# Starting gate/up of three column blocks on half of the rows, with fill matmuls and the first weights in one queue

## The chip, the cores and the metric

The kernel runs on 1 core of one Trainium2 chip. The metric is device time in microseconds (us); times are given as medians. Before the change the kernel takes 1308.88 us (3 runs, 1308.24 to 1309.98).

## The reference, cut to what matters

A layer norm, a multi-head attention over a cached K and V (32 heads of 128), and a gated feed-forward part whose result gates the attention output:

```python
xn = layernorm(x)                       # x: 2048 rows x 512
s  = attention(xn @ wq, k_cache, v_cache) @ wo
gate = xn @ W_gate                      # 512 x 1792
up   = xn @ W_up
h    = (gate * (gate > 0)) * up
g    = silu(h @ W_down)
out  = x + s * g
```

Everything is bfloat16 with fp32 accumulation. The feed-forward part is computed first, then the attention. The first matmul that does useful work needs normalised and transposed rows (`xnT`) and the first columns of `W_gate` and `W_up`.

## The kernel before

Rows are handled in four groups of 512 (`Q`), each of four tiles of 128 rows. The 1792 columns of gate and up are 14 blocks (`fc`). For the first 512 rows the head normalises and transposes all four tiles before the first gate matmul. Twelve dummy matmuls run first, to have TensorE's clock up: the traces record the clock that TensorE is granted, 1.00 or 0.50 (called warm and cold, or full and half, below). In the trace of this kernel a 512-column matmul starts every 0.216 us at 1.00 and every 0.43 us at 0.50.

```python
FCS = [0, min(2, FC), min(8, FC), FC]      # weight chunks: blocks 0-1, 2-7, 8-13
...
load_x0(sp, 0); load_x0(act, 1); load_x0(sp, 2); load_x0(act, 3)
load_w(sp, Wg_sb, wg_src, sem_wg, 0)       # first gate weights: SP queue
load_w(act, Wu_sb, wu_src, sem_wu, 0)      # first up weights: ACT queue
load_w(sp, Wg_sb, wg_src, sem_wg, 1)
load_w(sp, Wu_sb, wu_src, sem_wu, 1)
...
def head_ln():
    st = ln_stats(0)
    st = ln_stats(1)
    sq01 = ln_aggr([0, 1], st)             # square root on ACT
    st = ln_stats(2)
    c01 = ln_coef([0, 1], sq01)
    n0 = ln_norm(pool, sem_nm, 0, c01)     # GpSimd
    n1 = ln_norm(pool, sem_nm, 1, c01)
    st = ln_stats(3)
    sq23 = ln_aggr([2, 3], st)
    c23 = ln_coef([2, 3], sq23)
    n2 = ln_norm(dve, sem_ln4, 2, c23)
    n3 = ln_norm(dve, sem_ln4, 3, c23)
    head_transpose(0, n0, act, sem_xa)     # 4 TensorE transposes, then one copy to xnT
    head_transpose(1, n1, act, sem_xa)
    head_transpose(2, n2, act, sem_xa)
    head_transpose(3, n3, dve, sem_xt)
...
def emit_gate_up(Q):
    for fc in range(FC):
        s = ring_acquire()                 # one of 3 pairs of PSUM banks
        if fc == 0:
            _wait_all(pe, xt_ready[Q])     # all four tiles
        if Q == 0 and fc in FCS:           # a new chunk of weights
            k = FCS.index(fc)
            pe.wait_ge(sem_wg[k].h, 16)
            pe.wait_ge(sem_wu[k].h, 16)
        for c in range(DC):                # 4 gate matmuls of 512 columns
            pe.matmul(ps_r[:, gb, :], Wg_sb[:, c, fs], xnT[:, c, qs], ...)
        # ... 4 up matmuls, relu on ACT, product hT on DVE, one ln_task for later rows
...
for _i in range(12):
    pe.matmul(ps_acc[:, 0, 0:D], warm[:, 0:128], warm[:], start=True, stop=True)
head_ln()
for Q in range(QB):
    hlast = emit_gate_up(Q)
    if Q < QB - 1:
        emit_down(Q, hlast)
# ... attention of 32 heads; then the last output projection:
while oproj_queue:
    _, g_, n_ = oproj_queue.pop(0)
    emit_M(None, None, (g_, n_))
gL = NG - 1
for n in range(NT):
    if n == 0:
        _wait(pe, t_tok(gL))               # the last DMA transposes of the attention output
    # ... 4 matmuls, product and sum on DVE, store
```

The softmax here doesn't subtract the row's maximum and nothing guards it: scores larger than these inputs give would overflow.

Of the kernel before, what the change touches and what calls it, by code (L numbers as in the profile page):

```python
# [5 lines left out]
BF16 = mybir.dt.bfloat16  # L6
F32 = mybir.dt.float32
ALU = mybir.AluOpType
ACTF = mybir.ActivationFunctionType
# [20 lines left out]
def _wait(eng, tok):  # L30
    if tok is None:
        return
    sem, val = tok
    if val <= 0:
        return
    eng.wait_ge(sem.h, val)


def _wait_all(eng, toks):
    best = {}  # L40
    for t in toks:
        if t is None:
            continue
        sem, val = t
        k = id(sem)
        if k not in best or best[k][1] < val:
            best[k] = (sem, val)
    for sem, val in best.values():
        _wait(eng, (sem, val))


def bass_recurrent_scan__mha_block_cached__glu_gated_reglu__prompt_kernel(
# [12 lines left out]
    _, S, D = A_x.shape  # L65
# [8 lines left out]
    DC = D // 128  # L74
    FC = F // 128
# [8 lines left out]
    NSLOT = 3  # L84
# [13 lines left out]
    pe = nc.tensor  # L98
    act = nc.scalar
    dve = nc.vector  # L100
    sp = nc.sync
    pool = nc.gpsimd

    with ExitStack() as es:
# [13 lines left out]
        ps_r = P_([128, 2 * NSLOT, 512], F32, "ps_r")  # L118
        ps_acc = P_([128, 2, 512], F32, "ps_acc")
        acc_bf = [ps_acc[:, k, :].bitcast(BF16) for k in range(2)]  # L120

        x_sb = S_([128, NT, D], BF16, "x_sb")
        xnT = S_([128, DC, S], BF16, "xnT")
# [9 lines left out]
        warm = S_([128, D], BF16, "warm")  # L133
# [12 lines left out]
        Wg_sb = SB_([128, DC, F], BF16, "Wg_sb")  # L146
# [47 lines left out]
        with nc.Block() as block:  # L194

            @block.tensor
            def _(_pe_eng):
# [10 lines left out]
                for b in range(2):  # L208
                    tok_pool = sem_pool.sig(pool.memset(V_sb[b][:, :, Dh:VW], 2.0))

                FCS = [0, min(2, FC), min(8, FC), FC]
                wg_src = B_W_gate.rearrange("(c p) f -> p c f", p=128)
                wu_src = B_W_up.rearrange("(c p) f -> p c f", p=128)

                def load_w(eng, dst, src, sems, k):
                    a, b_ = FCS[k] * 128, FCS[k + 1] * 128
                    if b_ > a:
                        sems[k].sig(eng.dma_start(dst[:, :, a:b_], src[:, :, a:b_]))
# [14 lines left out]
                load_x0(sp, 2)  # L233
                load_x0(act, 3)
                load_w(sp, Wg_sb, wg_src, sem_wg, 0)
                load_w(act, Wu_sb, wu_src, sem_wu, 0)
                load_w(sp, Wg_sb, wg_src, sem_wg, 1)
                load_w(sp, Wu_sb, wu_src, sem_wu, 1)
                if QB > 1:
# [58 lines left out]
                def ring_acquire():  # L298
                    s = ring_cnt[0] % NSLOT
                    ring_cnt[0] += 1  # L300
                    _wait_all(pe, ring_tok[s])
                    ring_tok[s] = []
                    return s
# [8 lines left out]
                def ln_aggr(ns, stok):  # L312
                    _wait(dve, stok)
                    for n in ns:
                        atok = sem_ln2.sig(dve.bn_aggr(mv[:, n, :], stats[:, n, :]))
                    a, b_ = ns[0], ns[-1] + 1
                    _wait(act, atok)
                    if a == 0:
                        _wait(act, warm_tok)
                    return sem_sq.sig(  # L320
                        act.activation(sqv[:, a:b_, :], mv[:, a:b_, 1:2], ACTF.Sqrt, bias=eps_sb[:]))

                def ln_coef(ns, sqtok):
                    a, b_ = ns[0], ns[-1] + 1
                    _wait(dve, sqtok)
                    rtok = sem_ln3.sig(dve.reciprocal(rstd[:, a:b_, :], sqv[:, a:b_, :]))
                    _wait(dve, rtok)
                    return sem_ln3.sig(
                        dve.scalar_tensor_tensor(nmr[:, a:b_, :], mv[:, a:b_, 0:1], -1.0, rstd[:, a:b_, :],
                                                 op0=ALU.mult, op1=ALU.mult))  # L330

                def ln_norm(eng, sem, n, ctok):
                    _wait(eng, ctok)
                    return sem.sig(
                        eng.tensor_scalar(xn_sb[:, n, :], x_sb[:, n, :], rstd[:, n, 0:1], nmr[:, n, 0:1],
                                          op0=ALU.mult, op1=ALU.add))
# [1 line left out]
                xt_ready = {Q: [] for Q in range(QB)}  # L338

                def head_transpose(n, ntok, eng, sem):  # L340
                    tp_ps = ps_r[:, n, :].bitcast(BF16)
                    if n == 0:
                        _wait(pe, tok_pool)
                    _wait(pe, ntok)
                    ins = None
                    for c in range(DC):
                        ins = pe.transpose(tp_ps[:, c * 128:(c + 1) * 128],
                                           xn_sb[:, n, c * 128:(c + 1) * 128], ident[:])
                    ptok = sem_tp.sig(ins)
                    src = tp_ps[:, 0:DC * 128].rearrange("p (c q) -> p c q", c=DC)  # L350
                    _wait(eng, ptok)
                    copy = act.copy if eng is act else dve.tensor_copy
                    ctok = sem.sig(copy(xnT[:, :, n * 128:(n + 1) * 128], src))
                    xt_ready[0].append(ctok)
                    ring_tok[n // 2].append(ctok)

                def head_ln():
                    st = ln_stats(0)
                    st = ln_stats(1)
                    sq01 = ln_aggr([0, 1], st)  # L360
                    st = ln_stats(2)
                    c01 = ln_coef([0, 1], sq01)
                    n0 = ln_norm(pool, sem_nm, 0, c01)
                    n1 = ln_norm(pool, sem_nm, 1, c01)
                    st = ln_stats(3)
                    sq23 = ln_aggr([2, 3], st)
                    c23 = ln_coef([2, 3], sq23)
                    n2 = ln_norm(dve, sem_ln4, 2, c23)
                    n3 = ln_norm(dve, sem_ln4, 3, c23)
                    head_transpose(0, n0, act, sem_xa)  # L370
                    head_transpose(1, n1, act, sem_xa)
                    head_transpose(2, n2, act, sem_xa)
                    head_transpose(3, n3, dve, sem_xt)

                ln_hold = {}

# [23 lines left out]
                sig_free = [None, None]  # L400
                hT_free = [None, None]

                def emit_gate_up(Q):
                    qs = slice(Q * NQ, (Q + 1) * NQ)
                    par = Q % 2
                    h_tok = None
                    for fc in range(FC):
                        fs = slice(fc * 128, (fc + 1) * 128)
                        s = ring_acquire()
                        gb = 2 * s  # L410
                        if fc == 0:
                            _wait_all(pe, xt_ready[Q])
                        if Q == 0 and fc in FCS:
# [3 lines that stand above are left out]
                        ins = None  # L417
                        for c in range(DC):
                            ins = pe.matmul(ps_r[:, gb, :], Wg_sb[:, c, fs], xnT[:, c, qs],  # L419
                                            start=(c == 0), stop=(c == DC - 1))  # L420
                        gtok = sem_gate.sig(ins)
                        for c in range(DC):
                            ins = pe.matmul(ps_r[:, gb + 1, :], Wu_sb[:, c, fs], xnT[:, c, qs],  # L423
                                            start=(c == 0), stop=(c == DC - 1))
                        gu_tok = sem_gu.sig(ins)
                        gk = fc % NSLOT
                        _wait(act, gtok)
                        _wait(act, gr_free[gk])
                        rtok = sem_relu.sig(act.activation(gr_sb[gk][:], ps_r[:, gb, :], ACTF.Relu))  # L429
                        _wait(dve, gu_tok)  # L430
                        _wait(dve, rtok)
                        if fc == 0:
                            _wait(dve, hT_free[par])
                        h_tok = sem_h.sig(
                            dve.tensor_tensor(hT[par][:, fc, :], gr_sb[gk][:], ps_r[:, gb + 1, :], ALU.mult)  # L435
                        )
                        gr_free[gk] = h_tok
                        ring_tok[s] = [rtok, h_tok]
                        if Q == 0:
                            ln_task(fc)  # L440
                    return h_tok

                def emit_down(Q, h_last_tok):
# [27 lines left out]

                assert DC == 4 and FC >= 4 * (QB - 1) + 1
                _wait(pe, warm_w)
                for _i in range(12):
                    pe.matmul(ps_acc[:, 0, 0:D], warm[:, 0:128], warm[:], start=True, stop=True)
                head_ln()
                ring_cnt[0] = 2
                for Q in range(QB):
                    hlast = emit_gate_up(Q)
                    if Q < QB - 1:  # L480
# [294 lines left out]
```

## Time and profile before

| | before |
|---|---|
| median of 3 runs | 1308.88 us |
| profiled span | 1309.6 us |
| TensorE busy | 98% |
| first gate matmul | 9.28 us |
| half clock near the head | 9.51 to 12.93 us |
| first matmul of the down projection in the chain of work that ended last ("the chain") | 35.30 us |
| TensorE idle before the last output projection | 6.0 us |

From the page of the kernel before, the busy times of the engines and the head of the chain that ended last:

```profile
PE 1281.4 (98%) x11744; PEld 838.4 (64%) x11964; DVE 442.6 (34%) x1190; ACT 1000.7 (76%) x1107; POOL 11.5 (1%) x23
...
PE 93%; DVE 3%; issue 2%; DMA 1%; SPq 0%; ACTq 0%; DVEq 0%
```

TensorE is the bound. Next, the timeline of the head of the kernel before; columns are start, duration, engine, line, operation, tiles, shape, count, and in brackets the idle time just before and what ended it:

```profile
1.19 5.17 PE L475 MATMUL ps_acc<-warm 128*128 128x512 bf16 x12 [1.19 <-DVE warm L230]
...
3.21 1.29 DVE L310 BATCH_NORM_STATS2 stats<-x_sb 128x6 f32<-128x512 bf16 x2 [2.07 <-DMA x_sb<-in_A_x_dram]
...
5.72 1.52 POOL L335 TENSOR_SCALAR xn_sb<-x_sb,rstd,nmr 128x512 bf16<-128x512 bf16 x2 [4.03 <-DVE nmr L329]
...
6.63 0.38 PE L347 MATMUL ps_r<-ident,xn_sb 128*128 128x128 bf16 x4 [0.27 <-POOL xn_sb L335]
...
7.29 1.18 PE L347 MATMUL ps_r<-ident,xn_sb 128*128 128x128 bf16 x12 [0.28 <-POOL xn_sb L335]
...
9.28 1.66 PE L419 MATMUL ps_r<-xnT,Wg_sb 128*128 128x512 bf16 x4 [0.81 <-DMA Wu_sb<-in_B_W_up_dram]
```

Dummies end at 6.36 us; then only transposes, until the first gate matmul at 9.28 us, which the landing of the up weights released. The windows of the kernel before (stretch, its length, busy time and count per engine, then granted TensorE clock, DMA share, GB/s) show what followed:

```profile
8.00:9.00 1.00, 0.47 (x7) 0.23 (x4) 0.44 (x2) 0.80 (x2) 0.00 (x0) 1.00 1.06 386
9.00:10.00 1.00, 0.72 (x3) 0.35 (x4) 0.00 (x0) 0.00 (x0) 0.00 (x0) 0.76 1.03 372
10.00:11.00 1.00, 1.00 (x4) 0.33 (x3) 0.00 (x0) 0.02 (x1) 0.00 (x0) 0.50 1.07 366
11.00:12.00 1.00, 1.00 (x3) 0.29 (x2) 0.00 (x0) 0.58 (x1) 0.00 (x0) 0.50 1.09 366
12.00:13.00 1.00, 1.00 (x4) 0.42 (x3) 0.31 (x1) 0.00 (x0) 0.00 (x0) 0.54 1.07 374
```

The third number from the end is the clock. It falls to 0.50 just as useful work begins: four matmuls per us instead of seven. A clock of 1.00 before 6.1 us is not a measurement: the trace's first clock record begins there, and the dummies, 0.43 us apart, show that the array was cold.

### The profile page before, as it was taken

The numbers are of one execution on the slowest core, as the hardware profiler recorded it, in microseconds if no ns is written. First come the engines' busy times: TensorE is split into PE (matmuls) and PEld (weight loads), VectorE is DVE, ScalarE is ACT, GpSimd is POOL, SyncE is SP. The second block draws the span as 40 slices with busy tenths as digits, with TensorE's granted clock in tenths as the row PEclk, the third lists the DMA queues.
The fourth block names the chain that finished last, engine by engine and source line by source line (L and its number), as shares of the span: only waits on it lengthen the run. The fifth ranks groups of instructions, "written<-read, shape, count | busy, mean of one in ns | idle before, by whom it ended". The sixth has DMA issues, their size and how long they took to land.

```text
span 1309.6 us, 27449 instructions
## 1 busy us (share of the span) xinstructions
PE 1281.4 (98%) x11744; PEld 838.4 (64%) x11964; DVE 442.6 (34%) x1190; ACT 1000.7 (76%) x1107; POOL 11.5 (1%) x23
## 2 busy tenths in 40 slices
PE   9999999999999999999999999999999999999996
PEld 3444466666666666666666666666666666666663
DVE  6333322222332332233233233223323323344546
ACT  3322389998888888888888888888888888888880
POOL 2000000000000000000000000000000000000000
PEclk9999999999999999999999999999999999999998
DMA  8500112232222322232221222222223222212202
GB/s 254 116 1 1 21 37 51 46 61 41 45 51 53 70 51 52 53 68 53 52 52 40 57 42 51 52 70 53 52 52 69 51 53 53 50 44 43 48 18 70
DMA packets 251575, 71.82 MB, mean 55 GB/s; under 512 B 238400, under 2 KB 251456, under 8 KB 251456
## 3 DMA queue, kind: packets, MB, share of 16 engines
q1 hardware_dynamic: 250640, 69.55, 25.4%
q8 instruction: 95, 1.56, 0.5%
q10 hardware_dynamic: 816, 0.52, 0.1%
q14 instruction: 24, 0.20, 0.0%
HBM read 32.77 MB, written 2.10 MB: 27 GB/s over the span
## 4 chain that ended last, share of the span: by engine, by line
PE 93%; DVE 3%; issue 2%; DMA 1%; SPq 0%; ACTq 0%; DVEq 0%
PE ps_acc L652 36%; PE ps_r L589 32%; PE ps_r L524 7%; PE ps_r L545 7%; PE ps_r L423 4%; PE ps_r L419 4%; PE ps_acc L456 4%; DVE Onorm L617 2%; DVE fin_tmp L731 1%; DMA Wu_sb<-in_B_W_up_dram 1%; PE ps_r L726 0%; DVE rz_sb L610 0%; SPq L628 0%; DMA OT_store<-Onorm 0%; ACTq L224 0%
## 5 line engine op out<-in xcount | busy, mean ns | idle before, releaser
L597 ACT ACTIVATE PT<-ps_r 128x1024 bf16<-128x1024 f32 x1024 | 952.3, 1054 | 172.8 <-PE ps_r L589 172.8
L652 PEld LDWEIGHTS ps_acc<-V_sb,PT 128*128 128x128 bf16 x8192 | 551.8, 98 | 247.9 <-DVE Onorm L617 6.1
L652 PE MATMUL ps_acc<-V_sb,PT 128*128 128x129 bf16 x8192 | 640.3, 221 | 2.5 <-DVE Onorm L617 0.4
L589 PE MATMUL ps_r<-QT_sb,KT_sb 128*128 128x512 bf16 x1844 | 565.5, 379 | 10.6
L610 DVE RECIPROCAL rz_sb<-ps_acc 128x2 f32<-128x2 f32 x256 | 42.2, 165 | 736.9 <-PE ps_acc L652 710.6
L589 PEld LDWEIGHTS ps_r<-QT_sb,KT_sb 128*128 128x128 bf16 x2048 | 159.3, 98 | 1.1 <-DVE QT_sb L535 0.4
L617 DVE TENSOR_SCALAR Onorm<-ps_acc,rz_sb 128x128 bf16<-128x128 f32 x512 | 156.1, 347 | 9.2
L524 PE MATMUL ps_r<-xnT,Wq_sb 128*128 128x512 bf16 x511 | 130.8, 379 | 0.1
L545 PE MATMUL ps_r<-Wo_sb,OT_store 128*128 128x512 bf16 x447 | 114.8, 379 | 0.1
L524 PEld LDWEIGHTS ps_r<-xnT,Wq_sb 128*128 128x128 bf16 x512 | 50.1, 98 | 60.5
L535 DVE CAST QT_sb<-ps_r 128x512 bf16<-128x512 f32 x128 | 87.2, 681 | 0.7 <-PE ps_r L524 0.7
L545 PEld LDWEIGHTS ps_r<-Wo_sb,OT_store 128*128 128x128 bf16 x448 | 43.8, 98 | 52.6 <-DMA OT_store<-Onorm 0.2
L429 ACT ACTIVATE gr_sb<-ps_r 128x512 bf16<-128x512 f32 x56 | 33.4, 596 | 56.2 <-PE ps_r L419 53.5
L558 DVE TENSOR_TENSOR s_acc<-s_acc,ps_r 128x512 f32<-128x512 f32 x96 | 65.9, 687 | 12.3
L419 PE MATMUL ps_r<-xnT,Wg_sb 128*128 128x512 bf16 x220 | 57.7, 384 | 1.0 <-DMA Wu_sb<-in_B_W_up_dram 0.8
L423 PE MATMUL ps_r<-xnT,Wu_sb 128*128 128x512 bf16 x219 | 57.8, 384 | 0.3
L435 DVE TENSOR_TENSOR hT<-gr_sb,ps_r 128x512 bf16<-128x512 bf16 x56 | 38.5, 687 | 50.4 <-PE ps_r L423 46.6
L456 PE MATMUL ps_acc<-Wd_sb,hT 128*128 128x512 bf16 x220 | 48.8, 379 | 0.2
L419 PEld LDWEIGHTS ps_r<-xnT,Wg_sb 128*128 128x128 bf16 x224 | 22.0, 99 | 27.8 <-issue 1.1
L423 PEld LDWEIGHTS ps_r<-xnT,Wu_sb 128*128 128x128 bf16 x224 | 22.1, 99 | 27.1 <-issue 1.1
L462 ACT ACTIVATE sig_sb<-ps_acc 128x512 f32<-128x512 f32 x16 | 9.6, 597 | 38.8 <-PE ps_acc L456 36.4
L456 PEld LDWEIGHTS ps_acc<-Wd_sb,hT 128*128 128x128 bf16 x224 | 21.9, 98 | 26.5
(33 smaller groups left out, 128.1 us busy)
## 6 DMA issues: line engine op xcount, KB each, us to landing
V_sb<-in_A_v_cache_dram SPq DMA_DIRECT2D x32, 512.0 KB, 5.0
OT_store<-Onorm SPq DMA_TRANSPOSE x512, 2.4
Wq_sb<-in_A_wq_dram SPq DMA_DIRECT2D x32, 128.0 KB, 2.7
Wo_sb<-in_A_wo_dram SPq DMA_DIRECT2D x8, 512.0 KB, 4.2
Wd_sb<-in_B_W_down_dram SPq DMA_DIRECT2D x1, 1792.0 KB, 13.5
Wg_sb<-in_B_W_gate_dram SPq DMA_DIRECT2D x2, 768.0 KB, 9.4
Wu_sb<-in_B_W_up_dram SPq DMA_DIRECT2D x2, 768.0 KB, 10.4
x_sb<-in_A_x_dram SPq DMA_DIRECT2D x3, 512.0 KB, 10.8
```

The lines of the kernel that those rows point to most:

```text
L419: ins = pe.matmul(ps_r[:, gb, :], Wg_sb[:, c, fs], xnT[:, c, qs], start=(c == 0), stop=(c == DC - 1))
L423: ins = pe.matmul(ps_r[:, gb + 1, :], Wu_sb[:, c, fs], xnT[:, c, qs], start=(c == 0), stop=(c == DC - 1))
L456: ins = pe.matmul(ps_acc[:, jb, 0:D], hT[par][:, fc, j * 128:(j + 1) * 128], Wd_sb[:, fc, :], start=(fc == 0), stop=(fc == FC - 1))
L524: ins = pe.matmul(ps_r[:, bank, :], Wq_sb[b][:, c, :], xnT[:, c, qs], start=(c == 0), stop=(c == DC - 1))
L535: etok = sem_qpe.sig(dve.tensor_copy(QT_sb[b][:, qs], ps_r[:, bank, :]))
L545: ins = pe.matmul(ps_r[:, bank, 0:D], OT_store[g % 2][:, hh, n * 128:(n + 1) * 128], Wo_sb[g % 2][:, hh, :], start=(hh == 0), stop=(hh == ...
L558: dve.tensor_tensor(s_acc[:, n, :], s_acc[:, n, :], ps_r[:, bank, 0:D], ALU.add)
L589: ins = pe.matmul(ps_r[:, 2 * s + tt, :], KT_sb[h % 2][:, t * 128:(t + 1) * 128], QT_sb[h % 2][:, qs], start=True, stop=True)
L597: act.activation(PT[pb][:], ps_r[:, 2 * s:2 * s + 2, :], ACTF.Exp, scale=scale)
L610: rztok = sem_rz.sig(dve.reciprocal(rz_sb[:, bank, :, :], z_ap))
L617: dve.tensor_scalar(Onorm[ob][:, j, :], ps_acc[:, bank, base:base + Dh], rz_sb[:, bank, jj, :], None, op0=ALU.mult,)
L652: ins = pe.matmul(o_ap, PT[pb][:, tt, j * 128:(j + 1) * 128], V_sb[vb][:, t, :], start=(t == 0 and j % 2 == 0), stop=(t == KT - 1 and j % ...
```

## The change

The intent: let TensorE begin gate and up of three column blocks on the first 256 rows, while the next 256 rows are normalised, and do the second 256 columns of those blocks afterwards; keep TensorE busy in between with three dummy matmuls; put the first up weights behind the first gate weights in one queue. For that, the first norms move from GpSimd to DVE (VectorE), the transposes go into other PSUM banks, and the first weight chunk grows from two to three blocks. The core of the diff:

```diff
-FCS = [0, min(2, FC), min(8, FC), FC]
+FCS = [0, min(3, FC), min(8, FC), FC]
+HFC = 3
 ...
-load_w(act, Wu_sb, wu_src, sem_wu, 0)
+load_w(sp, Wu_sb, wu_src, sem_wu, 0)
 ...
 def head_transpose(n, ntok, eng, sem):
-    tp_ps = ps_r[:, n, :].bitcast(BF16)
+    tp_ps = acc_bf[n % 2]
+    _wait(pe, acc_free[n % 2])
 ...
+def warm_mm(k):
+    for _i in range(k):
+        pe.matmul(ps_r[:, 2 * NSLOT - 1, 0:D], warm[:, 0:128], warm[:], start=True, stop=True)
 ...
-    n0 = ln_norm(pool, sem_nm, 0, c01)
-    n1 = ln_norm(pool, sem_nm, 1, c01)
+    n0 = ln_norm(dve, sem_ln4, 0, c01)
+    n1 = ln_norm(dve, sem_ln4, 1, c01)
+    head_transpose(0, n0, act, sem_xa)
+    head_transpose(1, n1, act, sem_xa)
+    warm_mm(3)
     st = ln_stats(3)
     sq23 = ln_aggr([2, 3], st)
+    emit_half(0, range(HFC - 1), xt_ready[0][0:2])
     c23 = ln_coef([2, 3], sq23)
     n2 = ln_norm(dve, sem_ln4, 2, c23)
     n3 = ln_norm(dve, sem_ln4, 3, c23)
-    head_transpose(0, n0, act, sem_xa)
-    head_transpose(1, n1, act, sem_xa)
     head_transpose(2, n2, act, sem_xa)
     head_transpose(3, n3, dve, sem_xt)
+    emit_half(0, range(HFC - 1, HFC), [])
+    emit_half(1, range(HFC), xt_ready[0][2:4])
 ...
+def emit_half(k, fcs, toks):
+    hs = slice(k * 256, (k + 1) * 256)
+    for fc in fcs:
+        ...                                   # waits, ring slot on the first half
+        for i, W in enumerate((Wg_sb, Wu_sb)):
+            if k == 0 and fc == 0 and i == 1:
+                pe.wait_ge(sem_wu[0].h, 16)
+            for c in range(DC):
+                ins = pe.matmul(ps_r[:, 2 * s + i, hs], W[:, c, fs], xnT[:, c, hs],
+                                start=(c == 0), stop=(c == DC - 1))
 ...
-for _i in range(12):
-    pe.matmul(ps_acc[:, 0, 0:D], warm[:, 0:128], warm[:], start=True, stop=True)
+warm_mm(12)
```

(Cut: moving relu and product into a function that the three blocks share with the other eleven, the bookkeeping of which PSUM bank is free, and `ring_cnt[0] = 2`, which is no longer needed. PSUM is the memory that TensorE writes to.)

More of the change, by code (lines that the diff above doesn't have):

```diff
@@ L354, in head_transpose @@
                     xt_ready[0].append(ctok)
-                    ring_tok[n // 2].append(ctok)
+                    acc_free[n % 2] = ctok
+                def warm_mm(k):
+                    for _i in range(k):
+                        pe.matmul(ps_r[:, 2 * NSLOT - 1, 0:D], warm[:, 0:128], warm[:], start=True, stop=True)
                 def head_ln():
@@ L369, in head_ln @@
                     n3 = ln_norm(dve, sem_ln4, 3, c23)
-                    head_transpose(0, n0, act, sem_xa)
-                    head_transpose(1, n1, act, sem_xa)
                     head_transpose(2, n2, act, sem_xa)
                     head_transpose(3, n3, dve, sem_xt)
+                    emit_half(0, range(HFC - 1, HFC), [])
+                    emit_half(1, range(HFC), xt_ready[0][2:4])
+                half_slots = []
+                def emit_half(k, fcs, toks):
+                    hs = slice(k * 256, (k + 1) * 256)
+                    for fc in fcs:
+                        fs = slice(fc * 128, (fc + 1) * 128)
+                        if k == 0:
+                            if fc == 0:
+                                pe.wait_ge(sem_wg[0].h, 16)
+                            half_slots.append(ring_acquire())
+                        if fc == 0:
+                            _wait_all(pe, toks)
+                        s = half_slots[fc]
+                        for i, W in enumerate((Wg_sb, Wu_sb)):
+                            if k == 0 and fc == 0 and i == 1:
+                                pe.wait_ge(sem_wu[0].h, 16)
+                            ins = None
+                            for c in range(DC):
+                                ins = pe.matmul(ps_r[:, 2 * s + i, hs], W[:, c, fs], xnT[:, c, hs],
+                                                start=(c == 0), stop=(c == DC - 1))
+                            if k == 1:
+                                half_tok[(fc, i)] = (sem_gate if i == 0 else sem_gu).sig(ins)
+                half_tok = {}
                 ln_hold = {}
@@ L401, in _, with finish_gate_up @@
                 hT_free = [None, None]
+                def finish_gate_up(Q, fc, s, gtok, gu_tok):
+                    par = Q % 2
+                    gb = 2 * s
+                    gk = fc % NSLOT
+                    _wait(act, gtok)
+                    _wait(act, gr_free[gk])
+                    rtok = sem_relu.sig(act.activation(gr_sb[gk][:], ps_r[:, gb, :], ACTF.Relu))
+                    _wait(dve, gu_tok)
+                    _wait(dve, rtok)
+                    if fc == 0:
+                        _wait(dve, hT_free[par])
+                    h_tok = sem_h.sig(
+                        dve.tensor_tensor(hT[par][:, fc, :], gr_sb[gk][:], ps_r[:, gb + 1, :], ALU.mult)
+                    )
+                    gr_free[gk] = h_tok
+                    ring_tok[s] = [rtok, h_tok]
+                    if Q == 0:
+                        ln_task(fc)
+                    return h_tok
                 def emit_gate_up(Q):
                     qs = slice(Q * NQ, (Q + 1) * NQ)
-                    par = Q % 2
                     h_tok = None
@@ L408, in emit_gate_up @@
                         fs = slice(fc * 128, (fc + 1) * 128)
+                        if Q == 0 and fc < HFC:
+                            s = half_slots[fc]
+                            finish_gate_up(Q, fc, s, half_tok[(fc, 0)], half_tok[(fc, 1)])
+                            continue
                         s = ring_acquire()
@@ L425, in emit_gate_up @@
                         gu_tok = sem_gu.sig(ins)
-                        gk = fc % NSLOT
-                        _wait(act, gtok)
-                        _wait(act, gr_free[gk])
-                        rtok = sem_relu.sig(act.activation(gr_sb[gk][:], ps_r[:, gb, :], ACTF.Relu))
-                        _wait(dve, gu_tok)
-                        _wait(dve, rtok)
-                        if fc == 0:
-                            _wait(dve, hT_free[par])
-                        h_tok = sem_h.sig(
-                            dve.tensor_tensor(hT[par][:, fc, :], gr_sb[gk][:], ps_r[:, gb + 1, :], ALU.mult)
-                        )
-                        gr_free[gk] = h_tok
-                        ring_tok[s] = [rtok, h_tok]
-                        if Q == 0:
-                            ln_task(fc)
+                        h_tok = finish_gate_up(Q, fc, s, gtok, gu_tok)
                     return h_tok
@@ L473, in _ @@
                 _wait(pe, warm_w)
-                for _i in range(12):
-                    pe.matmul(ps_acc[:, 0, 0:D], warm[:, 0:128], warm[:], start=True, stop=True)
+                warm_mm(12)
                 head_ln()
-                ring_cnt[0] = 2
                 for Q in range(QB):
```

## The prediction

> **What bounds the kernel now.** TensorE. The page gives PE 98% busy and the chain that ended last is 93% PE. From 9.28 us on, the chain of waits is an unbroken run of matmuls through the feed-forward part (0.216 us per 512-wide matmul at full clock), so time saved before it should pass through to the end. The change touches only the first 1.3% of the span.
>
> **The head before, from the timeline.** Twelve dummy matmuls run from 1.19 to 6.36 us, 0.43 us apart (cold clock). The 16 transposes follow from 6.63 to 8.47 us, 219 ns each. The last copy to xnT ends at 8.93 us. The first gate matmul starts at 9.28 us, released by the DMA of W_up (7.5 us to landing, on the ACT queue). The windows view shows the granted clock at 1.0 until 9.52 us, 0.5 until 12.93 us, then 1.0. So eight matmuls run at 0.43 instead of 0.216 us: 1.7 us lost. The transposes' 219 ns against about 621 ns for cold 512-wide matmuls says that the dummies had warmed the clock by about 6.1 us, and that the thin stretch from 6.4 to 9.3 us lost it again. The Trainium skill, "TensorE: Matmul & The Clock Gate", Part 1, describes a free-running window of about 3.4 us that decides the clock; the trace agrees (9.52 to 12.93 is 3.41 us). The phase may differ from run to run, so this 1.7 us is probably not lost in every run; the three times spread as much (1308.24 to 1309.98).
>
> **The change, costed.**
> - Norms of tiles 0 and 1 go from GpSimd (0.77 us each) to DVE (0.41 each): ready at about 6.0 and 6.4 us. Two ACT copies (0.585 each) make the first 256 rows ready at about 8.0 us instead of 8.9 for all rows.
> - The second pair is later: its stats come after the norms, its square root waits behind the two copies (about 8.0), norms end near 9.5 us, its eight transposes run near 9.9 to 10.6 us, now inside the matmul stream instead of before it: about 0.7 us taken back.
> - Halves cost nothing extra: 48 matmuls of 256 columns at an estimated 0.11 us equal 24 at 0.216.
> - Weights in one queue: the bytes moved (windows view, 0.23 to 0.38 MB per us) put gate near 6.8 and up near 8.0 us, no longer the last wait.
> - Three dummies (0.65 us warm) fill the gap before 8 us.
>
> Sum: three column blocks finish, with a warm clock, at about 14.0 us; before it is 14.5 us warm and 16.3 us as profiled. Reordering is worth about 0.4 us and the clock 1.7 us where it is lost: I assume two thirds of runs, mostly cured. Expected gain: about 1.5 us of 1309, or 0.1%.
>
> **Predicted time 1307.4 us**, range 1305.8 to 1308.9. Chances: faster by over 2% 0.003, within 2% 0.994, slower by over 2% 0.003.
>
> **What would show it.** Right: the first gate matmul near 8.1 us; no granted clock of 0.5 from 9.5 to 12.9; down projection of the first rows starting near 33.0 us instead of 35.3; the first matmuls released by the xnT copy, not by a weight DMA. Wrong: weights landing after 8.5 us; PE waiting for xnT before the second half; ACT's relus or the hT products (0.69 us on DVE beside 0.69 us statistics) holding back blocks 3 to 5.
>
> **What would make it wrong.** A window still judged too idle: the clock then falls as before and only about 0.4 us, or nothing, is left. The other way, if the profiled clock loss is in every timed run, the gain is 2.1 us or more.

## The result, and the profile after

| | before | after |
|---|---|---|
| median, 4 runs each | 1309.16 us (1308.24 to 1309.98) | 1308.76 us (1308.00 to 1309.35) |
| profiled span | 1309.6 us | 1307.3 us |
| first gate matmul | 9.28 us | 8.26 us |
| down projection in the chain | 35.30 us | 33.10 us |

The ratio is 0.9997, 95% interval 0.9979 to 1.0014: the same.

The same lines of the page after:

```profile
PE 1290.2 (99%) x11991; PEld 840.0 (64%) x11991; DVE 443.1 (34%) x1192; ACT 1000.5 (77%) x1107; POOL 10.0 (1%) x21
...
PE 94%; DVE 4%; issue 1%; SPq 1%; DMA 1%; ACT 0%; DVEq 0%
```

(The larger busy time of PE is no more work: 220 matmul records were missing from the trace of before, as its 11744 matmuls against 11964 weight loads show.) The timeline of the head after the change:

```profile
1.19 4.77 PE L361 MATMUL ps_r<-warm 128*128 128x512 bf16 x12 [1.19 <-DVE warm L231]
...
3.62 1.28 DVE L311 BATCH_NORM_STATS2 stats<-x_sb 128x6 f32<-128x512 bf16 x2 [2.49 <-DMA x_sb<-in_A_x_dram]
...
6.07 0.74 DVE L336 TENSOR_SCALAR xn_sb<-x_sb,rstd,nmr 128x512 bf16<-128x512 bf16 x2
...
6.62 0.63 PE L349 MATMUL ps_acc<-ident,xn_sb 128*128 128x128 bf16 x8 [0.67 <-DVE xn_sb L336]
...
7.09 0.81 PE L361 MATMUL ps_r<-warm 128*128 128x512 bf16 x3
...
8.26 0.60 PE L403 MATMUL ps_r<-xnT,Wg_sb 128*128 128x256 bf16 x4 [0.36 <-ACT xnT L355]
...
10.01 0.61 PE L349 MATMUL ps_acc<-ident,xn_sb 128*128 128x128 bf16 x8
```

The first gate matmul is now released by the copy to `xnT`, and TensorE has no gap afterwards. The clock (windows after, same columns) stays at 1.00:

```profile
8.00:9.00 1.00, 0.74 (x7) 0.69 (x8) 0.58 (x3) 0.31 (x2) 0.00 (x0) 1.00 1.06 365
9.00:10.00 1.00, 1.00 (x11) 0.90 (x10) 0.48 (x2) 0.00 (x0) 0.00 (x0) 1.00 1.07 368
10.00:11.00 1.00, 1.00 (x15) 0.93 (x13) 0.34 (x1) 0.57 (x1) 0.00 (x0) 1.00 1.08 355
```

In the two profiles, 2.2 us are won by 33 us. That the whole span is 2.3 us shorter does not follow from the head alone, though. Read from the two traces, piece by piece:

| piece | before | after | difference |
|---|---|---|---|
| start to the first weight load of the down projection ("the mark") | 34.92 | 32.73 | -2.19 |
| mark to the end of the first group of four heads | 259.06 | 259.06 | 0.00 |
| the other seven groups | 987.21 | 988.09 | +0.88 |
| idle before the last output projection | 6.03 | 6.03 | 0.00 |
| last output projection to the end | 22.40 | 21.36 | -1.04 |

(The mark is read from the trace to 0.01 us; it precedes the matmul in the chain by 0.37 us.) The head's gain goes undiminished through the rest of the feed-forward part and a whole group of heads. Then 0.9 us are lost at boundaries of later groups, and 1.0 us is won in the tail, where the clock was cold for two windows in one profile and one in the other. So the question for the experiments: is the 2.2 us real in every run, and are the +0.9 and -1.0 part of the change?

### The profile page after: what moved, and what is told of

Its sections match the earlier page's. It is cut to its first block, busy times and chain, and to the rows that moved or that the text cites. A ratio compares the mean times of both kernels' runs of the same rounds, so it can differ in the third digit from the quotient of the medians.

```text
span 1307.3 us, 27724 instructions
## 1 busy us (share of the span) xinstructions
PE 1290.2 (99%) x11991; PEld 840.0 (64%) x11991; DVE 443.1 (34%) x1192; ACT 1000.5 (77%) x1107; POOL 10.0 (1%) x21
## 4 chain that ended last, share of the span: by engine, by line
PE 94%; DVE 4%; issue 1%; SPq 1%; DMA 1%; ACT 0%; DVEq 0%
PE ps_acc L694 35%; PE ps_r L631 33%; PE ps_r L566 7%; PE ps_r L587 7%; PE ps_acc L500 4%; PE ps_r L481 4%; PE ps_r L477 4%; DVE Onorm L659 2%; SPq L670 1%; DVE fin_tmp L773 1%; DVE rz_sb L652 0%; PE ps_r L403 0%; DMA OT_store<-Onorm 0%; PE ps_r L768 0%; DMA x_sb<-in_A_x_dram 0%
## 5 line engine op out<-in xcount | busy, mean ns | idle before, releaser
L631 PE MATMUL ps_r<-QT_sb,KT_sb 128*128 128x512 bf16 x2048 | 609.7, 380 | 0.0
L481 PE MATMUL ps_r<-xnT,Wu_sb 128*128 128x512 bf16 x212 | 54.4, 379 | 0.0
L477 PE MATMUL ps_r<-xnT,Wg_sb 128*128 128x512 bf16 x212 | 54.4, 379 | 0.0
```

Of the source, the lines that this page charges most:

```text
L477: ins = pe.matmul(ps_r[:, gb, :], Wg_sb[:, c, fs], xnT[:, c, qs], start=(c == 0), stop=(c == DC - 1))
L481: ins = pe.matmul(ps_r[:, gb + 1, :], Wu_sb[:, c, fs], xnT[:, c, qs], start=(c == 0), stop=(c == DC - 1))
L631: ins = pe.matmul(ps_r[:, 2 * s + tt, :], KT_sb[h % 2][:, t * 128:(t + 1) * 128], QT_sb[h % 2][:, qs], start=True, stop=True)
```

## The experiments

Theory A: the half clock at the head of before comes only in some runs, according to where the free-running window of the clock happens to lie (in every trace here the clock changes only in steps of 3.41 us from its first rise, and where this grid lies, its phase, differs from run to run); the change by itself is worth well under 2.2 us, and the rest of the difference between two profiles is chance. Theory B (rival): before loses its clock in every run, the 2.2 us is always won, and is lost again later. Eleven kernels ran; all gave correct results.

### The kernel before again

Edit: none but a comment.

> The kernel before, unchanged, to see what of its profile repeats. Mark: start of the first down-projection matmul, 35.3 us in the first profile of before and 33.1 us after the change. Theory A (the clock loss depends on where the free-running 3.41 us window happens to lie): another profile may show no half clock after 9 us, and then the mark is near 33.6 us. Theory B (the loss is in every run of before, and the 2.2 us won at the mark are lost again later): half clock for 3.4 us beginning between 8.5 and 11 us again, mark 35.1 to 35.5 us. Either way the ratio of the times to before is 1.000 within 0.001; its interval is the noise that all other runs have to be read against.

Measured: 1309.46 us (5 runs) beside 1309.74 us (9 runs) of the same kernel, ratio 0.9996 (0.9982 to 1.0009). The clock rose at 4.97 us and was not lost. Windows, same columns as above:

```profile
9.00:10.00 1.00, 1.00 (x5) 0.46 (x6) 0.00 (x0) 0.00 (x0) 0.00 (x0) 1.00 1.05 385
10.00:11.00 1.00, 1.00 (x7) 0.47 (x5) 0.10 (x1) 0.60 (x1) 0.00 (x0) 1.00 1.07 369
```

The mark was 33.30 us (33.7 in the chain), 1.6 us earlier than in the first profile of the same kernel. Theory B falls with this one look: the half clock is not in every run. A second thing came to light. From the chain of waits of this run (start, duration, what):

```profile
2.67 9.99 DMA Wu_sb<-in_B_W_up_dram
12.66 0.14 issue
12.79 1.02 PE ps_r L420 x4
```

With the clock kept, TensorE reached block 2 before the second chunk of up weights (landed 12.66 us) and waited; I work the wait out as 0.37 us, from the 24.32 us between first gate matmul and mark here against 23.95 in the third profile of this head (below). After the change the first chunk holds three blocks, so this wait cannot come at block 2. And the seven later groups took 988.24 us here against 987.21 in the first profile of the same kernel: the +0.9 us of the table above is within what an unchanged kernel does.

### Fill alone

```diff
 head_transpose(1, n1, act, sem_xa)
+fill_mm(2)
 head_transpose(2, n2, act, sem_xa)
 head_transpose(3, n3, dve, sem_xt)
+fill_mm(4)
```

> Before, with nothing moved, but two dummy matmuls after the transposes of tile 1 and four after those of tile 3, so that TensorE never idles for long between the first dummies and the first gate matmul. If the thin stretch is what loses the clock (both theories), no half clock from 9 to 13 us and the mark falls from 35.3 to about 33.8 us; the first gate matmul stays at about 9.3 to 9.5 us. If the clock is lost although TensorE is kept busy, mark near 35.3. Times: theory B says about 1.5 us less than before in every run, theory A about half of that or less, in the noise.

Measured: 1309.57 us (5 runs), ratio to before 1.0002 (0.9989 to 1.0014). No half clock; mark 33.56 us. But the clock rose at 3.87 us in this run, a phase in which the head of before might have kept it as well, so the profile alone does not show that the fill did it. The times do not show the 1.5 us that theory B asked for.

### The change without the three dummies

```diff
-    warm_mm(3)
```

> After, without the three dummies between the transposes of the second tile and the first gate matmul. If the dummies are what keeps the clock: half clock for 3.4 us somewhere from 8.5 to 13 us, mark near 34.5 us instead of 33.1. If starting the halves early is enough by itself (they fill the window from 8.2 us): clock stays at 1.0 and the mark is 33.1 us as with the dummies. I expect the second with a chance of 0.6. Times: within 0.1% of after.

Measured: 1308.53 us (5 runs), ratio to before 0.9991 (0.9978 to 1.0003). Rise at 5.89 us, a phase close to that of the first profile of before (6.10), and the clock was kept; mark 32.47 us. The early halves filled the window themselves. The three dummies were not needed here.

### The change again

Edit: none but a comment.

> The kernel after, unchanged, beside the kernel before on the same chip. Theory B: mark 33.1 us again within 0.3 and times 1 to 2 us below before. Theory A: mark 32.7 to 33.4 us, times 0.3 to 1.2 us below before. The shift against before should again shrink at the boundaries of the groups of four heads (about 300, 585, 730, 870, 1150 us) by some tenths of a us if that is systematic, and elsewhere or with the other sign if it is chance in the landing of the transposes by DMA.

Measured: 1308.35 us (5 runs), ratio 0.9991 (0.9978 to 1.0003), the difference of the means 1.3 us. Mark 32.36 us, clock kept with the rise at 5.94 us. The seven later groups took 986.82 us, so this time they were faster than in the first profile of before: the loss at group boundaries is chance in sign and size (986.8 to 988.3 us over all profiles).

Something held in all four profiles of this kernel's head (the one without the three dummies and the one with the tail filled, below, among them): the mark came 29.10 to 29.11 us after the start of the first statistics. That start, 3.15 to 3.62 us in all profiles, is set by the landing of the first 128 rows. With the change, everything in the head hangs on that DMA.

### The tail filled, before and after

The profiles showed a much clearer gap than the head: 6.0 us of idle TensorE before the last output projection, then a cold clock for one or two windows. The fill was tried there, in both kernels; this also removes the noise of the tail, and gives another look at both heads.

```diff
     emit_M(None, None, (g_, n_))
+sf = ring_acquire()
+for _i in range(26):
+    pe.matmul(ps_r[:, 2 * sf, 0:D], warm[:, 0:128], warm[:], start=True, stop=True)
 gL = NG - 1
```

> The kernel before with 26 dummy matmuls (26 x 0.216 = 5.6 us) in the 6.0 us in which TensorE waits for the last transposes before the final output projection; the head is untouched, so it is also a third look at the head of before. Tail: no half clock after 1280 us, and the time from the first final matmul to the end falls from 22.3-22.4 us (two cold windows) to about 20.4 us. Ratio to before about 0.9987. Head: theory A (clock lost in some runs only) says a mark of 33.2 to 33.6 us with no half clock, or 34.9 to 35.0 with it, depending on where the clock rises first: lost if it rises near 6.1 us (as in the first profile), kept if it rises before about 5.3 us.

> After with the same 26 dummies in the 6.0 us gap of the tail: both fills together. Head mark 32.3 to 32.8 us without half clock, whatever the phase; tail 20.4 us instead of 21.4 to 22.3. Ratio to before about 0.998, about 1 to 2 us below after. If the tail is bound by VectorE (1.06 us for each of 16 tiles) and not by the cold clock, the tail stays at 21.4 or more and the times are those of after.

Measured, on the same chip beside before (1309.93 us, 9 runs): before with the tail filled 1308.03 us (1307.71 to 1308.46), ratio 0.9984 (0.9971 to 0.9996); after with the tail filled 1307.10 us (1306.54 to 1307.86), ratio 0.9977 (0.9963 to 0.9991). Timeline of TensorE at the tail, before the change, without the fill:

```profile
1280.43 0.81 PE L545 MATMUL ps_r<-Wo_sb,OT_store 128*128 128x512 bf16 x3
1287.25 16.76 PE L726 MATMUL ps_r<-Wo_sb,OT_store 128*128 128x512 bf16 x63 [6.01 <-issue]
```

and with it:

```profile
1279.99 5.77 PE L710 MATMUL ps_r<-warm 128*128 128x512 bf16 x26
1286.17 13.97 PE L729 MATMUL ps_r<-Wo_sb,OT_store 128*128 128x512 bf16 x63 [0.40 <-issue]
```

The 63 recorded matmuls of the projection take 13.97 instead of 16.76 us. From the first of them to the end is 20.20 us in both filled kernels, against 22.40 and 21.36 without the fill in the two first profiles. The wait itself is unchanged (6.03 us); the dummies only sit in it.

Of all ratios here, only these two have an interval that lies clear of 1.

Two readings for the head. First, before with the tail filled kept its clock (rise at 4.48 us), mark 33.26 us, so of three profiles of this head one lost it. Its five runs lie within 0.75 us of each other and its profiled run kept the clock, so probably none of the five lost 1.6 us. The mean granted clocks agree for four of the five (0.999, 0.999, 1.000, 0.999; the fifth has 0.998 and stays open). This is an estimate: half clock for a time t lowers the mean by half of t over the span, which gives the recorded mean in all 13 profiles, so 0.999 leaves at most 3.9 us of half clock, and a lost window in the head (3.41 us) with the cold end of the kernel (0.4 to 3.6 us in the profiles) would hardly fit. Second, the two filled kernels differ by the change alone and have the smallest spread: means 1308.06 and 1307.11 us, a difference of 0.96 us with a standard error of 0.26 (worked out from the spread of five runs each). That is the best measure here of what the change is worth, in runs in which before mostly kept the clock.

### The parts, one at a time

First up weights in the SP queue, in the kernel before:

```diff
-load_w(act, Wu_sb, wu_src, sem_wu, 0)
+load_w(sp, Wu_sb, wu_src, sem_wu, 0)
```

> Before, with only the first up weights moved from the ACT queue to the SP queue (still two column blocks). They should land at about 7.5 to 8 us instead of 9.1, so the first gate matmul is released by the last xnT copy, at about 5.75 us after the first statistics start (it was 6.07 and 5.83 in the two profiles of before). Worth 0.1 to 0.3 us at the mark, no more, since all four copies bind right behind. Mark 30.0 to 30.1 us after the first statistics if the clock is kept (30.15 in before with the clock kept), 31.7 if it is lost.

Measured (one look, 1310.80 us): first gate matmul 6.14 us after the first statistics, mark 30.97. The up weights landed at 6.30 us, sooner than expected, and the first gate matmul was released by the ACT copy, as expected. But it was not earlier, because the clock fell at 8.10 us and the last transposes ran cold (four in 0.62 us). The mark came sooner than the 31.7 us expected for a lost clock, since 1.6 us of the cold stretch (8.10 to 11.51 us) lay before the first gate matmul at 9.69 us. So the clock was lost in a phase (rise at 4.68 us) that lies between two in which this sort of head kept it (4.48 and 4.97):

```profile
7.00:8.00 1.00, 0.72 (x8) 0.41 (x8) 0.73 (x4) 0.75 (x2) 0.57 (x1) 1.00 1.04 367
8.00:9.00 1.00, 0.94 (x9) 0.77 (x8) 0.35 (x2) 0.85 (x2) 0.00 (x0) 0.55 1.06 396
```

These two windows of that run show the fall from 1.00 to 0.55. Phase alone is not the rule, then. An early rise makes the twelve dummies run faster and end sooner, and a late landing of the first rows makes the gap behind them longer.

Norms of tiles 0 and 1 on DVE, in the kernel before:

```diff
-n0 = ln_norm(pool, sem_nm, 0, c01)
-n1 = ln_norm(pool, sem_nm, 1, c01)
+n0 = ln_norm(dve, sem_ln4, 0, c01)
+n1 = ln_norm(dve, sem_ln4, 1, c01)
```

> Before, with only the norms of tiles 0 and 1 moved from GpSimd (0.77 us each) to DVE (0.41 us each). Tiles 0 and 1 are ready earlier by about 0.4 to 0.8 us, but the statistics of tile 3 wait behind them on DVE, so tiles 2 and 3 come later by about 0.8 us, and the first gate matmul with them, since all 512 rows are needed: 6.3 to 6.7 us after the first statistics instead of 5.8 to 6.1. So this part alone costs about 0.5 us and pays only with the halves.

Measured (one look, 1312.96 us): first gate matmul 6.57 us after the first statistics, against 5.83 in the two profiles of before that kept the clock. As expected, this part alone costs 0.7 us. It also lost the clock (10.29 to 13.71 us).

The norms back on GpSimd, in the kernel after (the last diff reversed):

> After, with the norms of tiles 0 and 1 back on GpSimd (0.77 us each). In four profiles with the change, the mark (first down-projection weights) came 29.10 to 29.11 us after the start of the first statistics and the first gate matmul 4.64 us after it. Here the second norm is ready about 0.8 us later and two copies hang on it one by one, so first gate 5.1 to 5.3 us after the first statistics and mark 29.6 to 29.7. If instead the second pair (norms 2 and 3, the end of the first half) sets the pace, the mark stays at 29.1.

Measured (one look, 1309.70 us): first gate 5.25 us after the first statistics, mark 29.72. As expected, the faster norms are worth 0.6 us once the halves are there to use them.

The first up weights back on the ACT queue, in the kernel after:

```diff
-load_w(sp, Wu_sb, wu_src, sem_wu, 0)
+load_w(act, Wu_sb, wu_src, sem_wu, 0)
```

> After, with the first up weights (now 384 KB) back on the ACT queue. If the queue matters, they land at 9.5 us or later as in before (9.1 us for 256 KB), the first up matmul waits 0.5 to 1.2 us on that DMA, and the mark is 29.6 to 30.3 us after the first statistics. If the DMA engines share alike, they land before 8.6 us and the mark is 29.1.

Measured (one look, 1309.89 us): mark 30.59 us after the first statistics, 1.48 us worse than with one queue, more than expected, and by another wait than expected. From the chain of waits of this run:

```profile
1.66 7.63 DMA Wg_sb<-in_B_W_gate_dram
9.29 0.05 issue
9.33 2.07 PE ps_r L403 x16
```

Not the up weights but the gate weights came last: 7.6 us to landing instead of 5.1 in the first profile after. Two transfers in two queues shared the engines, and the one needed first was slowed by the one needed second. The Trainium skill, "DMA: Bandwidth & Descriptors", section "Issuing engines are not separate DMA queues", says that DMAs from different engines interleave on the same 16 engines; this trace agrees (7.63 against 5.1 us). So do the kernels with two blocks in the first chunk: their 256 KB of gate weights took 5.7 to 6.7 us in five profiles with two queues and 3.84 us in the one with one queue.

No dummies at all, in the kernel after:

```diff
-    warm_mm(3)
 ...
-warm_mm(12)
```

> After, without any dummy matmul (neither the first twelve nor the three). The clock is then cold when the halves start and rises only at the end of a window that holds about 1.3 us of matmul streaming (the boundary between the windows that kept the clock, 1.32 us and more, and those that lost it, 1.22 us and less, in the ten profiles so far): between 9.5 and 13 us. Half of the time from the first gate matmul to the rise is lost: mark 29.8 to 31.4 us after the first statistics instead of 29.1.

Measured (one look, 1311.23 us): the clock rose only at 12.66 us, mark 31.34 us after the first statistics. The dummies together are worth 2.2 us in that run. Since the run without the three dummies lost nothing, I put this down to the first twelve. Rise and mark lie in the expected ranges, but the reason given there does not hold: about 1.65 us of streaming in the window from 5.84 to 9.25 us, more than the 1.3 us named, did not raise the clock. What keeps it is not enough to raise it.

### What decides whether the clock is kept

For each profile I added up how long TensorE streamed in the first whole window after the clock had risen. This is an estimate: 0.213 us per matmul of 512 columns, in proportion for fewer, twice that at half clock. It follows from the pitch of 0.216 us in the traces and the formula of the Trainium skill, "TensorE: Matmul & The Clock Gate", "Back-to-back issue gap".

| head | window, us | streaming, us | of it transposes | clock after it |
|---|---|---|---|---|
| before, DVE norms | 6.88 to 10.29 | 0.88 | 0.62 | lost |
| before, first profile | 6.10 to 9.51 | 1.18 | 0.85 | lost |
| before, weights in one queue | 4.68 to 8.10 | 1.22 | 0.43 | lost |
| after, GpSimd norms | 4.12 to 7.53 | 1.29 | 0.21 | kept |
| before, tail filled | 4.48 to 7.90 | 1.32 | 0.43 | kept |
| before, fill alone | 3.87 to 7.29 | 1.42 | 0.21 | kept |
| before again | 4.97 to 8.38 | 1.51 | 0.85 | kept |
| after, weights in two queues | 6.95 to 10.37 | 1.61 | 0.11 | kept |
| after, without the three dummies | 5.89 to 9.30 | 1.90 | 0.43 | kept |
| after, tail filled | 4.59 to 8.00 | 1.92 | 0.43 | kept |
| after, first profile | 5.28 to 8.70 | 2.00 | 0.43 | kept |
| after again | 5.94 to 9.35 | 2.67 | 0.43 | kept |

Windows with up to 1.22 us of 3.41 (36%) lost the clock, windows from 1.29 us (38%) kept it. The row order is by streaming, and no other order that I tried sorts kept from lost: without the transposes, "before again" (0.66) kept it and "weights in one queue" (0.79) lost it; the summed records of busy TensorE do not sort them either (2.00 us lost in the first profile of before, 1.64 kept in the run with GpSimd norms). Nor does the longest pause of TensorE: 1.35 us in "before, tail filled" (kept), 1.32 us in "weights in one queue" (lost).

The rule is a fit to twelve windows; two of them, with GpSimd norms and with two queues, came after the boundary was on record and did not contradict it. No run was made to test it, but the traces hold a test: in all 13 profiles the last matmuls of the kernel end within a window, and none of those windows holds a transpose. Counted in the same way, seven of them held 0.36 to 1.00 us and lost the clock, six held 1.24 to 2.15 us and kept it for one window more. One of each kind, "before again" (0.95 us, lost) and "before, DVE norms" (1.24 us, kept), each with the window after it (same columns as above):

```profile
1302.03:1305.44 3.41, 1.12 (x6) 0.29 (x3) 3.27 (x8) 0.00 (x0) 0.00 (x0) 1.00 0.46 154
1305.44:1308.80 3.36, 0.00 (x0) 0.00 (x0) 1.43 (x3) 0.00 (x0) 0.00 (x0) 0.50 0.46 156
...
1303.95:1307.36 3.41, 1.41 (x7) 0.43 (x5) 3.31 (x7) 0.00 (x0) 0.00 (x0) 1.00 0.45 153
1307.36:1310.77 3.41, 0.00 (x0) 0.00 (x0) 1.68 (x4) 0.00 (x0) 0.00 (x0) 1.00 0.46 155
```

So the boundary lies near 1.2 to 1.3 us also where the fit did not look. Where in its record a matmul streams is not known, so single values are not sure to 0.1 us. What the rule says: the head of before sits near the edge (1.18 to 1.51 us), the head after sits above it (1.90 and more, except with GpSimd norms or two queues).

## Why the prediction was right or wrong

The time was right: 1308.76 us lies in the range, though near its upper end; 1.5 us was forecast, and 0.4 (first runs), 1.3 (the change again) and 0.96 us (tails filled, the best measure) were found. That the number was right says little: the range reached up to 1308.9 us, so no gain at all (1308.88 us before) would have been right too. The mechanism was right, two terms of the sum were mis-sized, and they partly cancelled.

- "the clock 1.7 us where it is lost: I assume two thirds of runs, mostly cured." The 1.7 us was right: from the first gate matmul to the mark it took 25.64 us with the clock lost and 23.95 us with it kept (first profile, and tail filled), 1.69 us. "Mostly cured" was right as far as seen: three profiles of the head after, and the one without the three dummies, kept the clock. **The share of runs is the term that was most off**, as far as these few looks go: one of three profiles of the unchanged head lost it, and probably none of the five timed runs with the tail filled. At one in seven, that is about 0.2 us on average, not 1.1. It is no count, though. Of the 18 further timed runs of before, two have a mean granted clock of 0.995, at least 11.8 us of half clock by the estimate above, where tail and end account for at most 10.4 us in the profiles; they most likely lost it too. For most of the others three figures do not decide.
- "Reordering is worth about 0.4 us". Measured from the start of the first statistics and with the clock kept, the mark is 29.78 us before (tail filled) and 29.11 after: 0.67 us, and 1.04 against the run in which before also waited for the second weight chunk, which I had not foreseen. In the first two profiles the 2.19 us at the mark are 1.69 us of clock and 0.91 us of this path, less 0.41 us because the first rows landed later in the profile after. The second pair of transposes takes 0.45 us in the stream (in the chain after, 10.17 to 10.62 us) and not 0.7, and the halves begin 4.64 us after the first statistics, 0.25 us sooner than I reckoned.
- "Halves cost nothing extra". Right: 48 of them run 0.109 us apart.
- "ready at about 6.0 and 6.4 us" and weights "near 6.8 and up near 8.0 us". Right: 1.68 + 5.1 us and 2.16 + 5.8 us. But I had the queue as a small matter; with the halves it is worth 1.5 us (two queues put back), since the halves need the weights 1.2 us sooner than the whole blocks did.
- "down projection of the first rows starting near 33.0 us instead of 35.3". Right in the profile (33.10), but that compared an unlucky run of before with a run of after.
- The spread of the three times (1308.24 to 1309.98) was set beside the loss of clock in the head. The profiles show more sources: 1.5 us of range in the seven later groups, about 1 us by one or two cold windows in the tail (one only where the first held 2.74 us of streaming, two in the ten profiles where it held 2.25 us or less), 0.5 us by the landing of the first rows.

Open: whether the three dummies ever matter. Without them the window in that one run still held 1.90 us; a phase in which they decide was not met.

## What to carry to other kernels

A warm-up whose count is fixed ends at a time that the clock decides; what counts is what TensorE does in the whole window after the rise, so look at a second profile before you price a cold stretch seen in one. Fill the gap that is really empty: 26 dummies in a 6 us wait won about 2 us here (2.3 us in the mean of the runs, 2.2 us in the tail of the trace), more than a careful reordering of a head (about 1 us), and both together made the fastest kernel (0.9977 of before). When two transfers are needed one after the other, put them in one queue in that order.

## What the Trainium skill lacked or had wrong

- "TensorE: Matmul & The Clock Gate" (Part 4) says that transposes do not count as TensorE activity the way other matmuls do. Here the run with 0.66 us of dummies and 0.85 us of transposes in its window kept the clock, and the one with 0.79 and 0.43 us lost it; that order fits only if transposes count for keeping it, and the windows at the end of the kernel, which hold none, lost the clock with up to 1.00 us of other matmuls.
- The same page (table "Why this matters for your kernels") has a cold clock after an idle window and warns of gaps over about 3 us. Here no gap in the heads that lost it was longer than about 1.5 us, and yet the clock was lost three times. The page gives no share: the windows here put it near 1.2 to 1.3 us of streaming in 3.41 us (an estimate, as said above).
- The page has one busy window as enough for the rise, without a share. By the same estimate, cold windows with up to 2.25 us of streaming did not raise it (the most in the tail of the first profile of before, from 1286.10 us; 1.65 us in the head without dummies), and those with 2.62 us (weights in one queue, 8.10 to 11.51 us) and more did.
- It agrees in the length of the window (9.51 to 12.93 us, 3.41 us before rounding) and in that the phase varies from run to run: the first rise came between 3.87 and 6.95 us in the kernels with dummies.
- "DMA: Bandwidth & Descriptors" says that two issuing engines share the DMA engines, but gives no number for what this does to the first of two transfers: 384 KB landed after 7.6 us beside a second queue and 5.1 us with the second transfer behind it.
